# Zeros products on TensorE with other banks and other counts, in a one-core attention and MLP kernel

## The chip, the cores and the metric

The kernel runs on one core of a Trainium2 chip. The metric is the device time of one execution in microseconds (us); lower is better.

## What is computed

Eight batches of a Nyström attention (8 heads, 576 tokens, head dimension 64, 32 landmarks), followed by a two-layer MLP with squared ReLU over all 4608 tokens (512 to 2048 to 512). Cut to what matters:

```python
q_lm = q.reshape(B, H, m, S // m, D).mean(axis=3)      # m = 32 landmarks
k_lm = k.reshape(B, H, m, S // m, D).mean(axis=3)
A, Bm, C = sm(q, k_lm), sm(q_lm, k_lm), sm(q_lm, k)    # scaled softmax
Z = Bm.T / (norm1(Bm) * norminf(Bm) + 1e-6)
for _ in range(6):
    Z = 2 * Z - Z @ Bm @ Z
x = A @ Z @ C @ v                                      # as (tokens, 512)
out = np.maximum(x @ w_in, 0.0) ** 2 @ w_out
```

## The kernel before

A planner collects operations. Each operation has a number, the engines that it may run on, and what it reads and writes. A list written out by hand, `ORDER`, then says in which order they are emitted and on which engine; every engine works through its own part of the list in order. A table, `PACE`, adds a few waits to loads and to work on GpSimd (POOL). The batches are staged so that the attention of batch b + 1 is mixed with the MLP of batch b. The attention of batch 0 has no such partner, so in the first 40 us TensorE (PE) has little work of its own.

PSUM is one tile, `ps`, of eight banks of 512 float32 columns. A non-negative entry of `ORDER` is 64 times the operation's number, plus 8 times the engine, plus the first bank that the operation's PSUM result gets. A negative entry -(8n + bank) stands for n zeros products: PE multiplies a 128x128 tile of zeros by itself into the first 128 columns of that bank. Nobody reads the result. Where the bank holds a result that another engine has still to read, the zeros wait for that reader, as any other writer of the bank would; and since PE works in order, all that stands behind them on PE waits with them.

The names in the profile, for batch 0 (and 1), in the order of their work:

- `tr`, `trk` (line 579): transposes of q and k by a permutation, six at a time into one bank; the copy `trev` (lines 304 on ACT and 306 on VectorE, DVE) takes them to qT and kT.
- `l_sum` (544), `l_ev` (310), `l_fold` (554), `l_dup` (304): landmark sums, to qls, kls and then qdup, kdup.
- `bmq_0` (604): landmark scores. They go through `nmb` (619), `Eb` (626), BB, BTf, cs, `mx` (645), cc and rc on DVE and ACT; `p0_0` (660) makes a first product of them, from BTc.
- `c_mm` (759): scores of landmark queries and all keys, then `nmc` (765, the maximum on DVE), `c_exp` (769), `c_tr` (781), `c_ev` (304, to ECT), `cv` (803).
- `nv_0` (689) and `upd` (704): the six iterations for Z. PE makes the product, DVE the update `st`, and the next product needs that update.
- `a_mm` (873), `a_t` (884, to SA), `a_max` (888), `a_sub` (890), `a_exp`, `a_mul` (901): scores of queries and landmark keys, their softmax.
- `g_mm` (929) and its copies to G, then `in_mm` (948), `relu` and `square` (965 to 975), `o_mm` (1020): the MLP.

In the core's first 40 us the loads of q, k, v and the weights are issued by POOL, in part after a wait that `PACE` sets on a result of DVE.

The zeros products come from this function:

Of the kernel before, what the change touches and what calls it, by code (L numbers as in the profile page):

```python
# [40 lines left out]
    592, 32, 344, 280, 472, 720, -583, 2628, 2309, 160, 784, 408, 200, 88, -55, 2182, 2248, -78, 1607, 1664, 2696,  # L41
    1736, 2368, 2440, 2758, 1560, 1796, 1864, 2887, 2952, -47, 3013, 984, 2832, 6016, 3088, 3208, 3144, 1496, 2052,
    9734, 1927, 2120, 6096, 920, 2501, 2568, 1368, 1992, 6594, 1176, 3280, 3344, 856, 3408, 3536, 3464, -39, 4992,
    9476, 6672, 3600, 5072, 1048, 5128, 1112, 3781, 3664, 3728, 3920, 3856, 9544, 4738, 4816, 4872, -77, 3975, 4048,
    -71, 4101, 6160, 5252, 4176, 5192, 6736, 4936, 1240, 4231, 4304, -71, 4357, 536, 4432, 5520, 5584, 5320, 5383,
    6232, 8772, 6280, 6352, 4485, 1432, 6808, 5448, -31, 5632, 4560, 4615, 9800, 6416, 9157, 6480, 5712, 1304, 4688,
    5890, 5760, 6856, 6928, 6992, 7064, 9606, 5968, 9216, 5832, 7168, 7240, 6544, 7362, 7312, 7432, 7120, 8024, 7960,
    -87, 7552, 7696, 7496, 7624, 8455, 15170, 656, 15360, 8216, 8512, 15248, 15312, 9288, 9349, 9424, 15432, 8584,
    18328, 15554, 15744, 15632, 18456, 9680, 15496, 18392, 18264, 9031, 15816, 9096, 15896, 8645, -39, 7746, 7824,
    15936, 7880, 16008, 16088, 8848, 8902, 8976, 16130, 16208, 8712, 8280, 15688, 16320, 16392, 9863, 8088, 9936,  # L50
    9992, 10056, 13826, 13904, 16456, 16512, 16584, 13250, 10128, 10192, 10256, 8152, 10312, 10392, 10448, 10512,
    16264, 13328, 10576, 13968, 22980, 23040, 16648, 23104, 16704, 16898, 16776, 16968, 8344, 21573, 21632, 8408,
    13392, 10694, 16840, 23168, 10640, 10832, 17088, 17160, 17282, 17352, 24720, 23232, 23296, 10896, 18759, 10768,
    10950, 17032, 17472, 21696, 13464, 12098, 17544, 26000, 11024, 18816, 18880, 18944, 13512, 25232, 17224, 11088,
    11142, 25296, 12176, 12296, 12232, 14040, 14088, 11216, 12352, 12432, 12552, 19008, 19072, 19136, 21760, 21824,
    11280, 11334, 19200, 19272, 21888, 25360, 25552, 21952, 25424, 23360, 12488, 11408, 25616, 11472, 22016, 22088,
    11526, 13584, 24792, 17666, 17736, 11600, 12743, 12614, 14160, 12816, 17856, 11672, 11717, 17928, 23424, 17416,
    20167, 20224, 12688, 12994, 25688, 25752, 17608, 12880, 11792, 25496, 12944, 11920, 11856, 11974, 24400, 14224,
    13072, 18048, 12048, 13125, 20288, 23496, 18120, 25816, 25872, 13648, 17992, 13200, 20352, 14402, 14472, 14592,
    14664, 14296, 14352, 20416, 20480, 13720, 24472, 14544, 24856, 14786, 14728, 14920, 14856, 20544, 20608, 13776,  # L60
    31488, 24536, 25104, 23558, 24920, 22148, 24600, 23616, 23680, 14978, 24984, 31560, 24664, 25040, 20680, 15112,
    25168, 15048, 26048, 26128, 26192, 26312, 26248, 23744, 19333, 34648, 19392, 17816, 34776, 25936, 20743, 20800,
    34712, 22208, 31682, 31872, 26384, 18184, 31752, 31632, 26448, 26512, 26704, 31944, 26768, 19456, 19520, 18648,
    19584, 19648, 28354, 28432, 31816, 18584, 28480, 18712, 19712, 26568, 26648, 28560, 20864, 20928, 28624, 28872,
    28808, 19776, 28744, 23808, 26832, 20992, 19856, 20064, 19936, 34584, 23872, 23936, 26896, 24000, 34840, 21056,
    21120, 24080, 27024, 20000, 22272, 22336, 26949, 27088, 27152, 28680, 21184, 32064, 32136, 42960, 42128, 35078,
    35136, 27205, 27280, 32008, 32258, 22400, 32328, 32448, 43032, 21264, 42192, 27344, 29061, 29200, 29264, 32520,
    32200, 22464, 22528, 32392, 42256, 42320, 27399, 27472, 30146, 27544, 30224, 18520, 21344, 29568, 29648, 42648,
    22592, 22672, 32584, 29128, 28935, 35200, 35264, 35328, 30288, 32642, 32832, 20128, 27589, 27664, 42712, 27736,
    32712, 35392, 29712, 36420, 36480, 29784, 32904, 32776, 33026, 33096, 42512, 33216, 33288, 36544, 36608, 27781,  # L70
    36672, 33160, 33410, 27856, 33600, 33480, 35456, 43088, 27920, 27973, 32976, 33672, 36736, 36800, 33360, 33794,
    33736, 42384, 28048, 28176, 28112, 33864, 33984, 24288, 35520, 30360, 41816, 41880, 34056, 41944, 42008, 29008,
    42072, 35584, 29832, 43344, 35648, 28229, 28304, 29314, 29392, 29904, 21472, 22816, 30408, 30480, 21536, 29968,
    21408, 37767, 30544, 22880, 37824, 33544, 30040, 37888, 30616, 34176, 34370, 34248, 29445, 42576, 29512, 34440,
    34504, 35712, 22944, 22752, 36864, 36928, 37952, 42776, 36992, 30912, 30722, 31048, 30792, 33928, 30992, 39109,
    35776, 30864, 39168, 39232, 39296, 31296, 31368, 31432, 31106, 31240, 37056, 37120, 31176, 37184, 38016, 35840,
    38080, 34136, 30096, 30672, 48896, 42832, 34320, 37248, 38144, 43152, 42896, 43216, 35904, 51992, 43280, 38208,
    38272, 52184, 42448, 48968, 43458, 43536, 49032, 43600, 43720, 43656, 45760, 37312, 37376, 37448, 35032, 45840,
    34968, 43792, 43856, 43920, 43984, 44056, 38336, 35968, 36032, 36104, 39360, 45890, 45968, 44112, 46032, 46216,
    44176, 24224, 46280, 39424, 39488, 39552, 52120, 38400, 38464, 37600, 38528, 38592, 44240, 44304, 44356, 44496,  # L80
    46152, 46088, 39616, 39680, 39744, 39808, 37536, 52056, 39872, 49090, 49160, 39936, 40000, 44432, 44568, 44614,
    43408, 57880, 46468, 46536, 49280, 49474, 52376, 38656, 49352, 49544, 40064, 44688, 38720, 44752, 49232, 37664,
    44806, 24160, 36320, 44880, 44944, 59024, 49664, 47554, 38792, 47632, 47696, 24352, 40452, 40512, 40576, 49736,
    49800, 40136, 44998, 49856, 49928, 50050, 49432, 34904, 46343, 50120, 50184, 40640, 40704, 46976, 46608, 49616,
    45072, 45144, 37728, 49992, 53829, 50242, 50312, 47056, 53888, 53952, 47120, 46416, 46672, 50432, 50504, 45190,
    45264, 52440, 54016, 50376, 38944, 50626, 47768, 50696, 58704, 54080, 54144, 39008, 45328, 57936, 36192, 39072,
    58192, 50816, 38880, 50888, 45383, 45456, 45584, 45520, 54208, 40768, 40832, 50576, 47816, 51010, 51080, 50760,
    46720, 47184, 45638, 36384, 58008, 36256, 59096, 46800, 52487, 52544, 47240, 51202, 40288, 51392, 51464, 40896,
    51272, 58264, 47888, 47952, 40960, 41024, 41088, 58776, 45712, 46854, 54272, 41152, 51584, 47312, 58328, 59160,
    47376, 47448, 46928, 50952, 48322, 48400, 40352, 51656, 48456, 54336, 51144, 52608, 52672, 52736, 48512, 48584,  # L90
    48130, 48200, 52800, 47504, 48656, 48272, 51336, 40224, 41216, 41280, 41344, 58840, 48704, 48840, 58072, 48776,
    55174, 51778, 51848, 51912, 54400, 52864, 52928, 41408, 48024, 48080, 59224, 64960, 52992, 58136, 55232, 53056,
    65032, 58384, 58456, 58904, 58968, 58576, 59288, 51536, 65154, 53120, 65224, 40416, 59344, 58512, 53184, 68248,
    58640, 59520, 59600, 54464, 65096, 54528, 54592, 59664, 51736, 59784, 59720, 59856, 68184, 65346, 65416, 68120,
    54656, 54720, 41480, 55296, 41632, 65536, 41696, 54784, 65608, 68056, 65730, 65800, 54856, 59920, 55360, 59984,
    60048, 55008, 53248, 53312, 60176, 41760, 60112, 60420, 55424, 61824, 60240, 60304, 60368, 60560, 60496, 41568,
    61954, 55488, 55552, 65288, 55616, 56516, 61904, 55680, 55744, 55808, 55872, 62032, 62096, 62216, 62152, 60632,
    60677, 62344, 55936, 65496, 52248, 59472, 52312, 53376, 60752, 56576, 53440, 56640, 56704, 53512, 60816, 56000,
# [989 lines left out]
```

## Time and profile before

| | |
|---|---|
| median of 3 runs | 265.64 us (264.98 to 266.68) |
| profiled execution | 266.57 us, its span 264.9 us |
| PE busy | 249.0 us (94%), 3007 matmuls |
| weight loads | 148.8 us (56%) |
| DVE, ACT, POOL busy | 202.6 us (76%), 201.1 us (76%), 146.5 us (55%) |
| zeros products (line 455) | 138, busy 13.0 us, 6.4 us of PE's idle time just before them |
| granted PE clock, mean over the span | 0.981 |

The span runs from the first to the last instruction of the profiled execution; its time has 1.67 us more around it. PE is the busiest engine. The zeros are a small part of the instructions and lie between 1.06 and 36.6 us. The idle time before them is counted as idle time of PE, and the name behind it is that of the instruction that ended it.

### The profile page before, as it was taken

How to read it: one execution, taken by the hardware profiler on the slowest of the kernel's cores; microseconds unless marked ns; L12 is line 12 of the kernel's file. 1: busy time of each engine (PE TensorE's matmuls, PEld its weight loads, DVE VectorE, ACT ScalarE, POOL GpSimd, SP SyncE). 2: the span in 40 equal slices, each digit the busy share in tenths (PEclk: the TensorE clock that was granted, in tenths of full speed). 3: DMA queues.
4: the chain of work that ended last, by engine and by line, in shares of the span. 5: the costliest groups of instructions: out<-in, count | busy, mean ns of one | idle time of the engine just before them, and what ended most of it. 6: DMA issues, size and time to landing. Idle time of an engine off the chain costs nothing.

```text
span 264.9 us, 7773 instructions
## 1 busy us (share of the span) xinstructions
PE 249.0 (94%) x3007; PEld 148.8 (56%) x3046; DVE 202.6 (76%) x488; ACT 201.1 (76%) x417; POOL 146.5 (55%) x219
## 2 busy tenths in 40 slices
PE   8768979999999999999999999999999999999995
PEld 8756755444664456454655466545645556466552
DVE  0075879999999779879989789799998967944521
ACT  1566489997999798996899599886787878665510
POOL 7236577587568664856687573945555345531000
PEclk9995799999999999999999999999999999999999
DMA  6999899908940795069622993096503431012232
GB/s 159 210 167 158 134 192 207 178 4 134 201 98 4 118 247 109 0 89 194 104 59 40 185 166 105 2 162 120 120 15 46 79 96 42 0 43 64 66 118 84
DMA packets 20470, 28.60 MB, mean 108 GB/s; under 512 B 3280, under 2 KB 11728, under 8 KB 20432
## 3 DMA queue, kind: packets, MB, share of 16 engines
q0 software_dynamic: 13296, 18.06, 43.5%
q1 hardware_dynamic: 6848, 9.77, 12.8%
q8 instruction: 24, 0.39, 0.6%
q10 hardware_dynamic: 288, 0.26, 0.3%
q14 instruction: 14, 0.11, 0.1%
HBM read 36.70 MB, written 9.44 MB: 174 GB/s over the span
## 4 chain that ended last, share of the span: by engine, by line
PE 80%; DVE 7%; ACT 6%; POOL 4%; issue 3%; DVEq 0%; ACTq 0%
PE ps L1020 40%; PE ps L948 21%; PE ps L455 4%; PE ps L725 3%; PE ps L926 2%; PE ps L781 2%; PE ps L544 2%; POOL EA L901 2%; PE ps L803 2%; ACT r L965 1%; PE ps L694 1%; ACT kT L304 1%; PE ps L579 1%; DVE nmc L765 1%; POOL ks L512 1%
## 5 line engine op out<-in xcount | busy, mean ns | idle before, releaser
L1020 PE MATMUL ps<-w_out_bf,gs 128*128 128x512 bf16 (+1 forms) x553 | 139.1, 373 | 3.3 <-issue 2.2
L1020 PEld LDWEIGHTS <-gs 128*128 128x128 bf16 x592 | 53.5, 98 | 47.3 <-issue 8.1
L948 PE MATMUL ps<-AT,G 128*128 128x288 bf16 x512 | 78.9, 286 | 0.8 <-issue 0.3
L965 ACT ACTIVATE r<-ps 128x576 bf16<-128x576 f32 x108 | 68.1, 651 | 13.0 <-PE ps L948 10.9
L948 PEld LDWEIGHTS <-G 128*128 128x128 bf16 x512 | 48.7, 98 | 24.2 <-issue 1.1
L973 ACT ACTIVATE gs<-r 128x576 bf16<-128x576 bf16 x83 | 55.4, 682 | 4.1 <-DVE r L967 3.5
L975 POOL TENSOR_TENSOR gs<-r 128x576 bf16<-128x576 bf16 x22 | 25.2, 1152 | 18.6 <-DVE gs L975 9.4
L304 ACT CAST G<-ps 128x512 bf16<-128x512 f32 x47 | 24.8, 592 | 5.5 <-PE ps L926 3.1
L379 POOL DMA_DIRECT2D vraw<-in_v_dram x32 | 18.2, 571 | 17.3 <-DVE BTf L633 9.0
L304 ACT COPY o<-ps 128x512 f32<-128x512 f32 (+1 forms) x32 | 18.0, 569 | 11.6 <-PE ps L1020 11.6
L967 DVE TENSOR_SCALAR r<-ps 128x576 bf16<-128x576 f32 x20 | 15.2, 762 | 10.2 <-PE ps L948 7.9
L455 PE MATMUL ps<-zero 128*128 128x128 bf16 x138 | 13.0, 265 | 6.4 <-ACT kT L304 2.9
L638 POOL TENSOR_TENSOR Pd<-st,ones_d 128x256 bf16<-128x256 bf16 x17 | 11.4, 671 | 12.2 <-DVE st L704 8.6
L890 POOL TENSOR_TENSOR SA<-SA,mxA 128x576 f32<-128x576 f32 x12 | 13.9, 1162 | 7.2 <-DVE qs L512 3.8
L746 ACT ACTIVATE EC<-ps,nmc 128x288 bf16<-128x288 f32 x24 | 11.7, 500 | 7.9 <-DVE nmc L739 6.3
L901 POOL TENSOR_TENSOR EA<-EA,rA 128x576 bf16<-128x576 bf16 x13 | 15.0, 1159 | 2.5 <-DVE rA L899 1.2
L533 DVE STREAM_TRANSPOSE qT<-qraw 128x1152 bf16<-128x1152 bf16 x12 | 16.4, 1364 | 0.0
L533 DVE STREAM_TRANSPOSE kT<-kraw 128x1152 bf16<-128x1152 bf16 x12 | 16.1, 1348 | 0.0
L455 PEld LDWEIGHTS <-zero 128*128 128x128 bf16 x138 | 11.5, 121 | 7.7 <-issue 6.1
L704 DVE SCALAR_TENSOR_TENSOR st<-st,ps 128x128 bf16<-128x128 bf16 x40 | 11.2, 279 | 4.8 <-PE ps L689 2.2
L306 DVE CAST G<-ps 128x512 bf16<-128x512 f32 x17 | 11.2, 677 | 3.2 <-PE ps L929 2.3
L884 DVE STREAM_TRANSPOSE SA<-ps 128x576 f32<-128x576 f32 x16 | 12.0, 768 | 1.4 <-PE ps L725 0.9
(146 smaller groups left out, 365.4 us busy)
## 6 DMA issues: line engine op xcount, KB each, us to landing
out_dram<-o SPq DMA_DIRECT2D x126, 64.0 KB, 3.0
qraw<-in_q_dram POOLq DMA_DIRECT2D x16, 288.0 KB, 6.0
vraw<-in_v_dram POOLq DMA_DIRECT2D x32, 144.0 KB, 5.6
kraw<-in_k_dram POOLq DMA_DIRECT2D x15, 288.0 KB, 6.5
w_in_bf<-in_moe_w_in_dram POOLq DMA_DIRECT2D x4, 512.0 KB, 7.8
w_out_bf<-in_moe_w_out_dram POOLq DMA_DIRECT2D x4, 512.0 KB, 8.5
out_dram<-o SPq DMA_DIRECT2D x3, 256.0 KB, 2.1
gs<-in_k_dram SPq DMA_DIRECT2D x2, 288.0 KB, 4.2
```

The costliest lines, as they stand in the source:

```text
L304: nc.scalar.copy(dst, src)
L379: nc.gpsimd.dma_start(vraws[z][p0:p0 + 32, :, :, :].rearrange("p g t d -> p g (t d)"), src[b].rearrange(order, i=2, t=SEG)[i, :, :, c * NJ ...
L455: mm(ps[:, bank, 0:P], lhsT=zero[:], rhs=zero[:], start=True, stop=True)
L533: add("hx", "DVE", lambda e, nm=nm, raw=raw, i=i: nc.vector.transpose(heads(nm)[:, i, :, :, :].rearrange("p t h r -> p (t h r)"), raw[:, i ...
L890: keep("a_sub", add("a_sub", "DVE POOL", lambda e, part=part, spread=spread: ENG[e].tensor_tensor(part(SA), part(SA), spread(part(mxA)), A ...
L901: keep("a_mul", add("a_mul", "POOL DVE", lambda e, part=part, spread=spread: ENG[e].tensor_tensor(part(EA), part(EA), spread(part(rA)), AL ...
L948: mm(t[:, j, 0:HALF], lhsT=G[:, i, f * P:(f + 1) * P], rhs=AT[:, i, j * HALF:(j + 1) * HALF], start=(i == 0), stop=(i == 1))
L965: nc.scalar.activation(r.rearrange("p (j t) -> p j t", j=2), src, AF.Relu)
L967: nc.vector.tensor_scalar(out=r.rearrange("p (j t) -> p j t", j=2), in0=src, scalar1=0.0, scalar2=None, op0=ALU.max)
L973: nc.scalar.activation(dst, r[:], AF.Square)
L975: ENG[e].tensor_tensor(dst, r[:], r[:], ALU.mult)
L1020: mm(one(ok)[:, 0:hi - lo], lhsT=gs[:, f, x0:x0 + P], rhs=w_out_bf[:, f, lo:hi], start=(f == f0), stop=(f == f1 - 1))
```

## The change

Only the negative entries of `ORDER` change; all the other entries, 2100 of them, stand in the same order with the same engines and banks. `PACE` stays. There were 11 runs of zeros with 138 products, and there are 16 with 143. With the entries just before and behind each run, and what stands behind it:

```diff
   472, 720,
-  -583,      # 72 into bank 7
+  -479,      # 59 into bank 7
   2628,      # tr, q of batch 0
...
   200, 88,
-  -55,       # 6 into bank 7
+  -63,       # 7 into bank 7
   2182, 2248,   # trk into bank 6, its copy on ACT
-  -78,       # 9 into bank 6
+  -86,       # 10 into bank 6
   1607,      # l_sum of k
...
   2887, 2952,   # tr into bank 7, its copy on ACT
-  -47,       # 5 into bank 7
+  -52,       # 6 into bank 4
   3013,      # bmq_0
...
   3536, 3464,
-  -39,       # 4 into bank 7
+  -44,       # 5 into bank 4
   4992,      # c_mm
...
   5128, 1112,
+  -15,       # 1 into bank 7
   3781,      # p0_0
...
   4816, 4872,
   -77,       # 9 into bank 5, as before
   3975, 4048,   # nv_0, upd
-  -71,       # 8 into bank 7
+  -68,       # 8 into bank 4
   4101, 6160,   # nv_0, a_max
+  -23,       # 2 into bank 7
   5252, 4176,   # c_tr, upd
...
   4231, 4304,
   -71,       # 8 into bank 7, as before
   4357,      # nv_0
...
   6808, 5448,
-  -31,       # 3 into bank 7
+  -39,       # 4 into bank 7
   5632,      # cv
...
   8024, 7960,
-  -87,       # 10 into bank 7
+  -95,       # 11 into bank 7
   7552,      # g_mm
...
   15896, 8645,
-  -39,       # 4 into bank 7
+  -46,       # 5 into bank 6
   7746,      # g_mm
...
   8902, 8976,
+  -15,       # 1 into bank 7
   16130,     # in_mm
...
   9992, 10056,
+  -44,       # 5 into bank 4
   13826, 13904, # a_mm of batch 1, a_t
   16456,
+  -20,       # 2 into bank 4
   16512,     # in_mm
```

272 rows, old and new, of the table ORDER are left out of this document.

## The prediction

> **What bounds the kernel now.** I read the page's engine shares and its 40 slices first. TensorE (PE) is busy 94% of the span, and nearly all that it lacks lies in the first 44 us, where the zeros products run; behind that, windows of 4 us show it 92 to 100% busy. So time won in the start should move everything behind it forward. Then I read PE's instructions in order of time (start, length, group; in brackets the idle time before it and what ended it):
>
> ```profile
> 1.06 6.28 PE L455 MATMUL ps<-zero 128*128 128x128 bf16 x72 [1.06 <-DVE zero L464]
> 7.17 0.50 PE L579 MATMUL ps<-perm,qraw 128*128 128x128 bf16 x6
> ...
> 8.35 0.50 PE L579 MATMUL ps<-perm,kraw 128*128 128x128 bf16 x6
> 9.73 0.66 PE L455 MATMUL ps<-zero 128*128 128x128 bf16 x9 [0.89 <-ACT kT L304]
> ...
> 13.57 0.44 PE L455 MATMUL ps<-zero 128*128 128x128 bf16 x5 [0.89 <-ACT qT L304]
> 13.94 0.23 PE L604 MATMUL ps<-kdup,qls 128*32 128x32 bf16 x8
> ...
> 16.92 0.38 PE L455 MATMUL ps<-zero 128*128 128x128 bf16 x4 [1.04 <-ACT kT L304]
> 17.23 0.33 PE L759 MATMUL ps<-kT,qdup 64*32 64x288 bf16 x12
> ...
> 20.90 1.01 PE L455 MATMUL ps<-zero 128*128 128x128 bf16 x8 [0.46 <-DVE st L704]
> 21.84 0.29 PE L689 MATMUL ps<-st 32*32 32x64 bf16 x8
> ...
> 36.20 0.38 PE L455 MATMUL ps<-zero 128*128 128x128 bf16 x4 [0.98 <-ACT kT L304]
> ```
>
> To see: the zeros (L455) do not fill the idle time, they come after it. Each run waits until another engine has read its bank, and then delays the real product behind it. Next, the order of time of all engines, for who reads which bank:
>
> ```profile
> 12.38 0.37 ACT L304 CAST kdup<-ps 128x256 bf16<-128x256 f32 x1
> ...
> 12.72 0.80 ACT L304 COPY qT<-ps 128x768 bf16<-128x768 bf16 x1
> ...
> 15.10 0.80 ACT L304 COPY kT<-ps 128x768 bf16<-128x768 bf16 x1
> ...
> 16.04 0.83 ACT L304 COPY kT<-ps 128x768 bf16<-128x768 bf16 x1
> ...
> 17.65 0.76 DVE L765 TENSOR_REDUCE nmc<-ps 128x1 f32<-128x576 f32 x1 [0.65 <-PE ps L759]
> ```
>
> The run at 13.57 waits for the copy at 12.72 (bank 7), that at 16.92 for the copy at 16.04 (bank 7 again). Last, busy time and granted clock by stretches (PE busy is the number after the length; PEclk stands behind POOL), and the landing of the first q load, issued at 1.34 us:
>
> ```profile
> 8.88:12.30 3.42, 2.57 (x46) 2.56 (x46) 0.00 (x0) 2.25 (x4) 0.00 (x0) 1.00 1.12 207
> 12.30:15.71 3.41, 2.52 (x55) 1.93 (x52) 1.90 (x6) 2.31 (x8) 0.00 (x0) 1.00 1.19 208
> 15.71:19.12 3.41, 1.68 (x51) 1.16 (x44) 2.56 (x10) 1.98 (x7) 1.86 (x3) 1.00 1.00 146
> 19.12:22.54 3.42, 2.96 (x38) 2.38 (x37) 2.03 (x6) 2.16 (x7) 2.54 (x5) 0.50 0.99 125
> 25.95:29.36 3.41, 3.41 (x116) 2.88 (x109) 3.21 (x9) 1.33 (x3) 1.31 (x2) 0.50 0.68 118
> 29.36:32.78 3.42, 3.42 (x60) 2.41 (x58) 2.30 (x5) 2.34 (x5) 2.13 (x3) 1.00 1.09 166
> ```
>
> ```profile
> qraw<-in_q_dram POOLq DMA_DIRECT2D x1, 288.0 KB, 5.1
> ```
>
> The clock is halved from 19.12 to 29.36 us, right behind the stretch in which PE was busy for only 1.68 of 3.41 us (49%); 74% kept it.
>
> **The change part by part.** Order, banks of the real products and added semaphore waits stay; only zeros change, 138 to 143; no DMA is issued from another place. In the rows a zeros product costs 107 ns start to start up to about 5.4 us, and 56 ns after.
>
> (a) First run 72 to 59: the 13 that go are late ones, 13 x 0.056 = 0.73, so the transposes start at 6.45 instead of 7.17. Their data lands at 1.34 + 5.1 = 6.44: just in time. But the k transposes at 8.35 need a load issued at 2.07 that takes 5.8 us, 7.87. They start at 7.9: gain 0.45, less 0.06 for one zero more at 9.73 (same bank, same wait). **0.39.** The seventh zero of the second run lies in the wait for k.
>
> (b) Run at 13.57, bank 7 to 4: bank 4's reader is kdup, which ends at 12.75, and the product behind needs kdup anyway. Six zeros then end 0.34 + 0.05 later, at 13.14 instead of 13.94. **0.80.** Nmb, Eb and the rest of ACT and DVE follow.
>
> (c) Run at 16.92, bank 7 to 4: bank 4's reader ends at 15.90, and the scores behind need qdup (15.77 + 0.39 = 16.16). PE could start about 1 us earlier, but next late is DVE: nmc stands there behind a transpose and mx, which ends at 17.01, so nmc moves from 17.65 to 17.0. **0.65.** The new single zero behind it hides in the wait for BTc (17.01), which ACT makes after reading that bank; uncovered 0.06.
>
> (d) Run at 20.90, bank 7 to 4: it waited for the update that the next iteration needs too, so all eight lay on the path. Bank 4's reader (qT) ends at 19.75, so they run during the update. PE gains 0.94, but DVE has a_max (20.76 to 21.51) ahead of the next update, which moves from 22.18 to 21.51. **0.67.** The two new zeros behind hide in the wait for EC.
>
> (e) Runs at 19.10 (9) and 23.39 (8) keep bank and wait. Three and then four zeros ahead of cv end about when ECT does; DVE is later there anyway. The run of ten, now eleven, at 30.42 lies beside the G copy that ends at 31.13. Cost 0; the two extra zeros uncovered, 0.11.
>
> (f) Run at 36.20, bank 7 to 6: bank 7's reader ends at 36.14, bank 6's (DVE qT, 34.99 + 0.55) at 35.54. Gain 0.60 less one zero: **0.54.** ACT's and DVE's G copies were waiting for it.
>
> (g) Eight new zeros (1, 5, 2) after that: five lie in PE's idle 0.66 ahead of 39.72, two in the idle 0.31 ahead of 40.94, one beside a copy. Cost 0; uncovered 0.45.
>
> Waits: 0.39 + 0.80 + 0.65 + 0.67 + 0.54 = **3.05 us**.
>
> (h) The clock. The trace of before can't show whether it stays up. Between 12.30 and 20.14 PE is busy for 5.22 of 7.84 us; the same work, some 4.8 us with zeros at full speed, then fits in 5.8, 82%. The next 8.2 us hold 7.37 of busy time at half clock, about 4.4 at full, in some 6.8: 65%, between the 49% that lost the clock and the 74% that kept it, nearer the latter. So I take a full clock. Worth, on the path: nine zeros 1.01 to 0.50 (DVE has 0.7 idle there), eight at 23.39 the same way 0.47, transposes and sums from 28.37 to 29.86, 1.49 to about 1.05. **1.4**; bounds 0 (half clock as before) to 4 (half of the 7.37, if all were on the path).
>
> (i) The loads. Their issues follow DVE and move along, but the stream runs near 200 GB/s from 30 to 52 us and can only move into its holes: 16 to 18 us (118 GB/s, some 0.9 us lost) and 28 to 30 us (24 GB/s, 1.8 us). The q and k loads of the third batch land 1.9 and 2.6 us before they are used, so most of it is covered. I take **0.5** back; bounds 0 and 1.8.
>
> Sum: 3.05 + 1.4 - 0.5 = 3.95, so 264.9 becomes about 260.9. The profiled execution took 266.57 with 1.67 around the span, which would become 262.6. It lay 0.93 above the median of the runs (265.64), so against that median: 265.64 - 3.95 = **261.7**. A change under 1% (2.66 us) can hardly be told from none here.
>
> **The rivals.**
> *The half clock stays.* The longer fillings do not reach what keeps the clock; then 3.05 - 0.5 = 2.55 remain: 263.1. For it: 65% is untested. Against: the lull before 19.12 shrinks. The Trainium skill, "TensorE: Matmul & The Clock Gate", "What's actually happening", has the clock halved after an idle window of about 3.4 us; the trace disagrees, since it halves behind a window 49% busy. Its section "A second HAM failure mode: psum-queue depth-cycling" has small gaps between groups toggle the clock, which would make this rival likelier, and the trace bears that out.
> *The loads set the pace.* The stream moves only by its holes, 0.9 + 1.8 = 2.7: 262.9. For it: 193 to 211 GB/s between 36 and 48 us. Against: 1.9 us of slack before use.
> *Slower: the half clock moves later.* It decides if PE, now ahead, meets its thin stretch near 24 to 26 us, so that the three windows fall on the projections (L948, from 32 us before) instead of the small products. Those 10.2 us hold some 7.5 us of PE path work at full clock, which doubles, less 1.6 idle: +5.9. Only the waits' 3.05 is won: 265.64 + 2.85 = 268.5. Against: at half clock the projections fill PE fully, and one full window (25.95 to 29.36) brought the clock back.
> *The banks are not freer*, and the zeros wait as before: 265.6. Against: every new reader ends earlier in the rows above.
>
> **How the numbers follow.** Forecast 0.63, half clock 0.14, loads 0.12, slower 0.05, no effect 0.06. Faster by over 1% (under 263.0): forecast nearly whole (0.60), half of the two at 263 (0.13): 0.73. Slower by over 1%: 0.05. Between: 0.22. The range: below, a clock worth 1.9 more than taken and no loss to the loads, 259.3; above, the rivals near 263 and the 1.7 by which the runs of before lie apart, 264.8. No effect and slower stay outside.
>
> **What would show it.** Right: zeros directly behind the kdup copy, the k transposes at about 7.9, the first projection (32.04) near 28, a granted clock of 1.00 between 19 and 29 us. Wrong: idle time before L455 as long as now; a clock of 0.50 past 29 us; DMA waits on DVE's khalf or qT near 40 us.

## The result, and the profile after

The changed kernel took 262.37 us in the median of four executions (262.20 to 262.94); the kernel before took 265.31 us on the same chip (264.36 to 266.68). The ratio is 0.9889, with a 95% interval from 0.9842 to 0.9937: some 2.9 us faster, and the forecast was 261.7. The profiled execution took 262.38 us with a span of 260.7 us, against 266.57 and 264.9; its span is 4.2 us shorter, and the forecast's sum was 3.95. That the two profiles lie further apart than the medians is told below, under (h). Two single executions further down, of 980.72 and 1390.87 us, lie far outside all others and are left out of every mean and ratio.

PE after, in order of time, in the same columns as before:

```profile
1.06 6.22 PE L455 MATMUL ps<-zero 128*128 128x128 bf16 x59 [1.06 <-DVE zero L464]
7.12 0.50 PE L579 MATMUL ps<-perm,qraw 128*128 128x128 bf16 x6
...
8.35 0.50 PE L579 MATMUL ps<-perm,kraw 128*128 128x128 bf16 x6
...
12.87 0.49 PE L455 MATMUL ps<-zero 128*128 128x128 bf16 x6
13.29 0.23 PE L604 MATMUL ps<-kdup,qls 128*32 128x32 bf16 x8
...
15.29 0.44 PE L455 MATMUL ps<-zero 128*128 128x128 bf16 x5
15.66 0.33 PE L759 MATMUL ps<-kT,qdup 64*32 64x288 bf16 x12
...
18.53 0.62 PE L455 MATMUL ps<-zero 128*128 128x128 bf16 x8
19.08 0.24 PE L689 MATMUL ps<-st 32*32 32x64 bf16 x8
...
27.62 1.02 PE L948 MATMUL ps<-AT,G 128*128 128x288 bf16 x7
...
31.86 0.44 PE L455 MATMUL ps<-zero 128*128 128x128 bf16 x5 [0.38 <-DVE qT L306]
```

To see: the brackets ahead of the three runs that moved to bank 4 (12.87, 15.29 and 18.53) are gone. The zeros now lie in the time that PE would have idled, and bmq_0 (L604) starts at 13.29 instead of 13.94, the scores (L759) at 15.66 instead of 17.23, the second product of the iteration (L689) at 19.08 instead of 21.84. The run ahead of the last g_mm still waits, 0.38 instead of 0.98 us. But the first run, 13 zeros shorter, ends when the old one did: the transposes start at 7.12 (7.17 before) and those of k at 8.35 in both.

The granted clock by stretches, cut at the same times as before (PE's busy time stands behind the length, the clock behind POOL's):

```profile
15.71:19.12 3.41, 2.54 (x69) 1.93 (x72) 3.04 (x10) 2.53 (x8) 2.43 (x5) 1.00 1.09 162
19.12:22.54 3.42, 2.54 (x58) 2.00 (x58) 2.50 (x8) 2.85 (x9) 3.26 (x5) 1.00 1.06 135
22.54:25.95 3.41, 3.40 (x132) 2.59 (x131) 3.34 (x10) 1.49 (x4) 1.50 (x3) 1.00 1.19 196
```

The clock stays at 1.00 where it was halved from 19.12 to 29.36 us before. And a new wait, from the order of time of all engines:

```profile
29.17 0.61 PEld L544 LDWEIGHTS <-kraw 128*128 128x128 bf16 x9 [0.71 <-DMA kraw<-in_k_dram]
```

The bracket says that the weight load for the landmark sums of batch 1 waits for its k. That load was issued at 20.95 us instead of 23.44, but took 8.0 us to land instead of 5.3: 29.0 against 28.8 us. Whether k was really what PE waited for is taken up under (i) below.

### The profile page after: what moved, and what is told of

The parts are those of the page before. It is cut to its first block, busy times and chain, and to the rows that moved or that the text cites. A ratio compares the mean times of both kernels' runs of the same rounds, so it can differ in the third digit from the quotient of the medians.

```text
span 260.7 us, 7783 instructions
## 1 busy us (share of the span) xinstructions
PE 246.9 (95%) x3012; PEld 147.2 (56%) x3051; DVE 202.1 (78%) x488; ACT 201.1 (77%) x417; POOL 146.4 (56%) x219
## 4 chain that ended last, share of the span: by engine, by line
PE 79%; DVE 8%; ACT 4%; issue 4%; POOL 4%; DVEq 0%; ACTq 0%
PE ps L1020 40%; PE ps L948 21%; PE ps L455 4%; PE ps L725 3%; PE ps L926 2%; POOL EA L901 2%; PE ps L544 2%; PE ps L781 2%; PE ps L803 2%; PE ps L694 1%; DVE SA L884 1%; ACT r L965 1%; POOL ks L512 1%; PE ps L579 1%; DVE nmc L765 1%
## 5 line engine op out<-in xcount | busy, mean ns | idle before, releaser
L304 ACT CAST G<-ps 128x512 bf16<-128x512 f32 x47 | 24.8, 592 | 4.6 <-PE ps L926 3.1
L975 DVE TENSOR_TENSOR gs<-r 128x576 bf16<-128x576 bf16 x23 | 10.2, 450 | 3.5 <-ACT r L965 3.3
```

The source lines that it names most:

```text
L304: nc.scalar.copy(dst, src)
L975: ENG[e].tensor_tensor(dst, r[:], r[:], ALU.mult)
```

## The experiments

Runs of zeros are written as bank and count; an edit names the work that stands behind the run. All comparisons are with the kernel before on the same chip; a ratio is not exactly the quotient of the two medians beside it. The first four experiments ran on one chip, the next four on another, the last four on a third, and the changed kernel itself was not run again beside them. So where another kernel is set against the changed one, the ratios count more than the medians.

**All four bank moves, no count changed.**

```diff
-bmq_0: bank 7, 5    c_mm: bank 7, 4    second nv_0: bank 7, 8    last g_mm: bank 7, 4
+bmq_0: bank 4, 5    c_mm: bank 4, 4    second nv_0: bank 4, 8    last g_mm: bank 6, 4
```

> The kernel before with four runs of zeros moved to another bank and nothing else: the five ahead of bmq_0 and the four ahead of the first c_mm go to bank 4, the eight behind the first nv_0 to bank 4, the four ahead of the last g_mm of batch 0 to bank 6. All counts stay, 138 zeros. Theory (the waits are the gain): about 2.9 us less than before from the four runs, and the clock, if it stays at 1.00 with these counts, another 1; so 261.5 to 262.5 where before is 265.3. Rival (the counts, through the clock, are the gain): no more than 0.5 us, 264.8 or over, with a stretch of clock 0.50 as before.

Measured: 262.77 us, before 265.52; ratio 0.9893 (0.9849 to 0.9938). The banks alone bring nearly all of it, as the theory of the waits says; the median ended 0.3 above the expected stretch. The clock stayed up in all six executions.

**All counts and the new runs, old banks.**

```diff
 counts 59, 7, 10, 6, 5, 1, 9, 8, 2, 8, 4, 11, 5, 1, 5, 2 as in the changed kernel
-bmq_0: bank 4    c_mm: bank 4    second nv_0: bank 4    last g_mm: bank 6
+bmq_0: bank 7    c_mm: bank 7    second nv_0: bank 7    last g_mm: bank 7
```

> All counts and the five new runs of the changed kernel, but the four runs keep the bank that they had before (bank 7). Theory (the waits are the gain): PE idles about 1 us ahead of each of these runs, as before, and the time is 264.5 to 265.5, at most 0.4 us below before from the shorter first run. Rival (the counts are the gain): 262.4, like the changed kernel.

Measured: 264.65 us, before 265.52; ratio 0.9982 (0.9946 to 1.0017). Its PE rows (the list is a few lines longer here, so zeros stand at L464):

```profile
13.10 0.50 PE L464 MATMUL ps<-zero 128*128 128x128 bf16 x6 [0.89 <-ACT qT L313]
...
16.50 0.44 PE L464 MATMUL ps<-zero 128*128 128x128 bf16 x5 [1.04 <-ACT kT L313]
...
20.03 0.61 PE L464 MATMUL ps<-zero 128*128 128x128 bf16 x8 [0.46 <-DVE st L713]
...
33.07 0.44 PE L464 MATMUL ps<-zero 128*128 128x128 bf16 x5 [0.98 <-ACT kT L313]
```

The same waits as before, to the hundredth. More zeros behind such a wait fill nothing; the rival falls. The counts alone do not hold the clock either: it was halved in 4 of the 12 executions (mean clock 0.98 to 0.994).

**The changed kernel without the zeros between 16 and 23 us.**

```diff
-p0_0: 1   first nv_0: 9   second nv_0: 8   c_tr: 2   fourth nv_0: 8   cv: 4
```

> The changed kernel without the zeros ahead of p0_0, the first two nv_0, c_tr, the fourth nv_0 and cv (1 + 9 + 8 + 2 + 8 + 4 = 32 zeros left out). What the zeros are worth through the clock: if they hold the clock, a stretch at 0.50 comes back behind 19 us and the time is 1 to 3 us above the changed kernel (263.5 to 265.5). Rival: the clock holds without them, and since 17 of them lie on the path between an update and the next product, the time is 0.5 to 1 us below (261.5).

Measured: 262.58 us (262.00 to 262.98); ratio 0.9882 (0.9842 to 0.9921), the same as the changed kernel. Both guesses missed the size, and half of each was right. The clock by stretches:

```profile
12.75:16.16 3.41, 3.34 (x85) 2.41 (x86) 2.87 (x9) 2.83 (x9) 1.30 (x3) 1.00 1.18 208
16.16:19.58 3.42, 1.39 (x45) 0.81 (x41) 3.25 (x10) 2.79 (x10) 2.29 (x6) 1.00 1.06 169
19.58:22.99 3.41, 2.96 (x111) 2.48 (x112) 2.58 (x9) 3.04 (x6) 2.67 (x3) 0.50 1.08 145
22.99:26.40 3.41, 3.41 (x46) 2.25 (x44) 2.31 (x8) 0.42 (x3) 2.52 (x3) 0.50 1.23 205
```

With PE busy for 1.39 of 3.42 us the clock is lost, in every one of six executions (mean clock 0.985 to 0.993). But the 17 zeros ahead of the first and fourth nv_0 no longer stand in the path: the fourth update comes at 20.38 instead of 21.61 us (0.46 of that is there already at nmb), and this pays for the half clock. At the first projection this kernel, though 0.46 ahead at nmb, is behind (28.07 instead of 27.62 us). It wins that back near 29 us, where PE pauses in the changed kernel and not here (see (i)). So in these two traces the zeros hold the clock, and up to the first projection they bring more than they cost; at the end the two kernels are even.

**72 zeros in the first run of the changed kernel.**

```diff
-first run: bank 7, 59
+first run: bank 7, 72
```

> The changed kernel with 72 instead of 59 zeros in the first run. Theory: the 13 late zeros cost 0.056 us each while the clock is full, 0.7 us, of which the wait for the k load at 7.8 us takes back a part, so 0.3 to 0.7 us above the changed kernel (262.7 to 263.1). Rival: the moment at which the clock is granted decides alone, and the time is within 0.2 us of the changed kernel.

Measured: 263.27 us; ratio 0.9910 (0.9871 to 0.9950), 0.0021 above the changed kernel's, about 0.55 us. That lies in the expected stretch, but it does not show the theory: the two intervals overlap, and the four moves alone, which also begin with 72 zeros, had 0.9893 on this chip. In the profiled execution the clock was granted at 5.21 us; the transposes start at 7.05 and those of k at 8.28, no later than in the changed kernel (7.12 and 8.35), as the rival says. Its span is still 0.9 us longer (261.6), because PE pauses for 1.18 us near 28 us instead of 0.52 (see (i)) and then waits 0.7 us for w_out.

**Four more runs in free banks.**

```diff
-l_sum of k: bank 6, 10   first nv_0: bank 5, 9   fourth nv_0: bank 7, 8   cv: bank 7, 4
+l_sum of k: bank 0, 10   first nv_0: bank 7, 9   fourth nv_0: bank 5, 8   cv: bank 2, 4
```

> The changed kernel with four more runs of zeros in banks that nobody has still to read: the ten behind the first k copy go to bank 0, the nine ahead of the first nv_0 to bank 7, the eight ahead of the fourth nv_0 to bank 5, the four ahead of cv to bank 2. Theory (waits ahead of zeros are time on the path until the loads take over): the first projection comes 1 to 1.8 us earlier than in the changed kernel, but the load stream, which PE already waits for near 29 us, takes most of it back; the end is 0 to 0.6 us earlier (261.8 to 262.4). Rival (the loads only cost that one wait): the end is 1.2 to 1.8 us earlier (260.6 to 261.2).

Measured: 261.03 us (260.10 to 261.98); ratio 0.9839 (0.9797 to 0.9881). Its slowest execution is faster than the fastest of the changed kernel, though on another chip, and the intervals of the two ratios overlap; between the ratios lie 1.3 us, as the rival said. In the profiled execution the first projection starts at 25.89 instead of 27.62 us, and the end of the span moves from 260.7 to 258.3. PE shows no wait for a load here, and the pause near 29 us is not there either: that is 0.67 of the 2.4 us.

**A lighter load stream.** A part of v of batch 0 is not loaded, so its result is incomplete.

```diff
-load_v of batch 0: 4 loads of 144 KB
+load_v of batch 0: 2 loads of 144 KB, the tile zeroed once on DVE
```

> The changed kernel with two of the four loads of v of batch 0 left out (144 KB each; their part of v is zero, so a part of batch 0's result is left out). Some 1.4 us less work for the load stream at 200 GB/s. Theory (the stream caps the gain between 27 and 40 us): no DMA wait on PE in that stretch, and the end is 0.5 to 1.2 us before the changed kernel. Rival (the stream is hidden): the same time within 0.3 us.

Measured: 261.95 us; ratio 0.9879 (0.9839 to 0.9919), 0.0010 below the changed kernel's, about 0.3 us: the same, by the rival's measure. But PE was not free of loads, as the theory wanted: it waited 0.6 us for w_in and 0.7 us for w_out. So this run does not settle what the loads are worth.

**Both together.**

> Both of the above: the four more free banks and the lighter load stream (part of v of batch 0 left out). Theory (stream and waits in turn set the pace): here the free banks show their worth, 1.5 to 2.5 us below the changed kernel (260 to 261), and more below the light kernel alone than the free banks gain with all loads. Rival (free banks are worth nothing because DVE's chain is the pace): the same as the light kernel alone.

Measured: 261.21 us; ratio 0.9858 (0.9815 to 0.9900). No better than the free banks with all loads, and 0.7 below the light kernel; PE waited 1.0 us for w_out at 35.6 us. Leaving out 288 KB does not make the later loads land earlier than they are needed, so this edit did not do what it was to do.

**Free banks, and 50 zeros in the first run.**

```diff
-first run: bank 7, 59
+first run: bank 7, 50
```

> The kernel with four more free banks, and 50 instead of 59 zeros in the first run. The first q load lands at about 6.1 to 6.5 us. Theory: 59 zeros end between 6.0 and 7.6 us, as the clock happens to be granted early or late, so 50 remove the late cases: 0 to 0.3 us earlier than with 59, since the k load at 7.8 us and the load stream behind it still hold the rest. Rival: with fewer zeros the clock is granted a window later, PE runs at half speed up to 8.9 us or loses it near 19 us, and the time is 0.5 us or more above that with 59.

Measured: 261.36 us (260.24 to 262.52); ratio 0.9843 (0.9781 to 0.9905): no gain that shows over 59. Where PE waits in the profiled execution:

```profile
PE ps L929 <- DMA w_in_bf<-in_moe_w_in_dram: 1.6, 1, 1.6
PE ps L455 <- DVE zero L464: 1.1, 1, 1.1
PE ps L579 <- DMA kraw<-in_k_dram: 1.0, 1, 1.0
PE ps L579 <- DMA qraw<-in_q_dram: 0.8, 1, 0.8
```

PE reaches the q and k transposes before their data. And the third w_in load, issued at 17.2 us, lands at 27.1, while it landed at 24.8 when issued at 16.7 with 59 zeros. The same load took 9.9 us here and 8.1 there; with PE this far ahead such a difference becomes a wait, and it likely lies behind the spread of the time here.

**The four moves one by one, on the kernel before.** The first two together:

```diff
-bmq_0: bank 7, 5   c_mm: bank 7, 4
+bmq_0: bank 4, 5   c_mm: bank 4, 4
```

> The kernel before with two runs moved to bank 4 and nothing else: the five ahead of bmq_0 and the four ahead of the first c_mm. Theory (each wait is worth what its term said): 0.8 + 0.65 = 1.45 us below the executions of before with the same granted clock (264.7 at a clock of 1.00, 266.6 at 0.98), and in the trace nmc (17.65 before) 1.4 us earlier if PE starts as then. Rival (DVE's chain behind it gives it back): under 0.5 us.

Measured: 263.82 us, before 265.89; ratio 0.9948 (0.9916 to 0.9979). At a mean clock over 0.99 the executions average 263.6, before 264.8: 1.2 us of the 1.45. The profiled execution is the one of 980.72 us, so where nmc stands was not seen. The third:

```diff
-second nv_0: bank 7, 8
+second nv_0: bank 4, 8
```

> The kernel before with the eight zeros behind the first nv_0 in bank 4 instead of 7. Theory: 0.67 us below before at the same clock; in the trace the zeros start within 0.1 us of nv_0's end and the next update follows a_max without idle time on DVE. Rival: the softmax work on DVE and POOL sets the pace there, and nothing is gained.

Measured: 265.20 us; ratio 0.9997 (0.9966 to 1.0027). At a mean clock over 0.99, 264.8 against 264.8. The local part came true in kind: the second update starts 0.87 us after the first, right behind a_max. But it took 1.17 us with the old bank and a full clock (20.86 after 19.69 us in the experiment with the counts), so at full clock the move is worth 0.30 us, not 0.67. The interval of the ratio is 1.6 us wide, so the time can't show whether these 0.30 us reach the end. The fourth:

```diff
-last g_mm: bank 7, 4
+last g_mm: bank 6, 4
```

> The kernel before with the four zeros ahead of the last g_mm of batch 0 in bank 6 instead of 7. Theory: the idle time ahead of them falls from 0.98 to 0.38 us and the end comes 0.5 to 0.6 us earlier at the same clock. Rival: the loads for the second stage (36 to 52 us) hold the rest, and the end does not move.

Measured: 265.29 us; ratio 0.9985 (0.9953 to 1.0017); 264.8 at a mean clock over 0.99, as before. Where PE waits:

```profile
PE ps L455 <- DVE qT L306: 0.4, 1, 0.4
PE ps L929 <- DMA w_in_bf<-in_moe_w_in_dram: 0.4, 1, 0.4
PE ps L1020 <- DMA w_out_bf<-in_moe_w_out_dram: 0.3, 1, 0.3
```

The wait ahead of the zeros fell from 0.98 to 0.38 as expected, and in this execution two waits for weights stand in its place, as the rival says. The interval leaves room for the 0.5 us of the theory too, so the time decides nothing.

**Six more runs in free banks.**

```diff
-second nv_0: bank 4, 8   last g_mm: bank 6, 5
+second nv_0: bank 5, 8   last g_mm: bank 2, 5
```

> The kernel with four more free banks (measured at 261.03 us) and two more: the eight zeros behind the first nv_0 go to bank 5, the five ahead of the last g_mm of batch 0 to bank 2. Theory (waits are still the pace): the idle 0.25 and 0.38 us ahead of these two runs goes, 0.3 to 0.6 us below 261.0. Rival (the loads, whose landing times differ by up to 2 us from run to run, now set the end): 260.8 to 261.4, with a spread of 1.5 us or more.

Measured: 260.27 us (259.62 to 263.78); ratio 0.9829 (0.9778 to 0.9880), the fastest median here, though hardly below the four free banks by the ratio (0.9839). Four executions lie between 259.62 and 260.32, as the theory of the waits wants; two at 262.84 and 263.78, as the rival's spread wants. The profiled one is the 262.84. Its stretches:

```profile
33.20:36.62 3.42, 1.72 (x23) 1.01 (x24) 2.98 (x11) 3.20 (x10) 1.16 (x2) 1.00 1.18 211
36.62:40.03 3.41, 3.36 (x14) 1.77 (x14) 1.08 (x3) 1.37 (x3) 2.72 (x4) 0.50 1.11 211
```

PE waited 1.4 us for a w_out load, was busy for only 1.72 of 3.42 us, and then ran at half clock for 3.4 us over dense work. A late load costs twice here.

## Why the prediction was right, and where not

**(b), (c), the early waits: right.** In the two traces bmq_0 comes 0.65 us earlier (forecast 0.80 less one zero more on the way, which the first run was to pay for), and nmc 1.37, so another 0.72 (forecast 0.65).

**(d), the iteration: the mechanism right, the price partly the clock's.** The second update comes 0.76 us more forward than the first (0.67). But the 1.01 us for eight zeros was read where the clock was halved. From the first to the second update it is 1.63 us in the trace before, 1.17 with the old bank at full clock (all counts, old banks) and 0.87 with the new bank (the changed kernel). So the bank is worth 0.30 of it, and the clock the other 0.46.

**(a), the first run: right in the mean, wrong as a fixed price.** I cut 13 zeros at 0.056 us each, taking the clock to be granted at 5.4 us as in the one trace I had. In the profile after, it was granted at 6.88 us; more zeros ran at 107 ns, and the shorter run ended at the same time: nothing of the 0.39 came. In other executions here it was granted between 3.7 and 6.9 us. The Trainium skill says as much ("TensorE: Matmul & The Clock Gate", "What's actually happening"): the activity window of 3413 ns runs freely and doesn't start with the kernel. These traces agree: the stretches of half clock last 3.41, 6.83 or 10.24 us, one, two or three such windows. The k transposes start at 7.99 us in the mean of the seven traces with 59 zeros (7.71 to 8.35) and at 8.40 in that of the five with 72 (7.74 to 8.83), 0.4 us apart where I had 0.45; a single execution tells little.

**(h), the clock: the mechanism right, the term mis-sized both ways.** In the two traces the clock brought more than the 1.4 us: 0.46 between nmc and the first update (0.50), 0.47 at the fourth product (0.47), and 1.35 instead of 0.44 between the fourth update and the first projection. That last stretch takes 7.36 us before and 6.01 after, and 6.01 also with the second nv_0 alone, which has the old zeros there and a full clock. My term covered only its end, from 28.37 us on. Together that is 2.28, besides the 0.46 that I had put under (d).

Against the median I took too much, since I took the 1.4 us from an execution in which the clock was halved. In the 57 executions of the kernel before that stand beside the experiments, 26 have a mean clock under 0.99 and average 266.4 us; the other 31 average 264.7. So an execution with the half clock is 1.7 us longer, but fewer than half have it: that is worth about 0.8 on the average of all. In none of the 23 executions of the changed kernel, of the four moves alone, of the 72 zeros and of the four more free banks was the clock halved.

Set against its own profiled execution the sum was right to 0.25 us (3.95 for 4.2). That is partly luck: that execution ran at a mean clock of 0.981, like the 26, and there the 0.39 of (a) that did not come and the 0.88 that the clock brought beyond its term point in opposite ways. Against executions with a full clock my terms, with 0.30 for (d), give 0.39 + 0.80 + 0.65 + 0.30 + 0.54 - 0.5 = 2.18; the changed kernel's 262.4 lies 2.3 below 264.7, though not on the same chip.

**(i), the loads: the size close, but by luck, since the wait was most likely another.** I looked for it at the q and k of the third batch near 40 us. It came near 29 us: the work around it is 4.41 us earlier just ahead of that wait (DVE's first relu, 32.80 to 28.39) and 3.74 just behind it (ACT's, 33.22 to 29.48), 0.67 against the 0.5 taken. The bracket names k of batch 1. But PE stands still already at a matmul that doesn't read k, the first line below, and "issue" says that it waited for nothing that the profile shows. The others are the four moves alone, the 72 zeros and the second nv_0 alone (their source lines are numbered a little differently):

```profile
29.16 0.28 PE L948 MATMUL ps<-AT,G 128*128 128x288 bf16 x1 [0.52 <-issue]
29.36 0.77 PE L956 MATMUL ps<-AT,G 128*128 128x288 bf16 x5 [0.83 <-issue]
28.56 0.49 PE L553 MATMUL ps<-perm,kraw 128*128 128x128 bf16 x6 [1.18 <-issue]
29.39 0.77 PE L948 MATMUL ps<-AT,G 128*128 128x288 bf16 x5 [0.52 <-issue]
```

In the last three no wait for k is named. In all four, PE stops behind exactly 479 matmuls and 480 weight loads, and goes on 1.35 to 1.43 us after a block of 16 KB has landed on the DMA queue that the page calls "q8 instruction" (27.76 us in the changed kernel). In the other nine traces the 480th matmul comes 1.48 us or more behind that landing, and PE doesn't stop. So it most likely waited for its own instructions, and a kernel that is ahead, or has more zeros by then, runs into it. No run changed how instructions are fetched, so this is read from the traces and not tested. Loads do become waits elsewhere: PE waits for w_in or w_out with the lighter stream, with 50 zeros, with six more free banks and with the last g_mm alone.

**(f): right.** G's copies come 4.28 us earlier, so about 0.54 was won again, as forecast (0.54), and 4.2 us are left at the end of the span. With this move alone, no gain could be told from noise. **(e)** cost nothing: the 6.01 us from the fourth update to the first projection are the same with the old and the new counts. **(g)** cost 0.1 us at most, what is lost from 4.28 to the end.

**The first projection** moves by 4.42 us, to 27.62, the "near 28" of the forecast.

**The rivals.** The banks were freer, as the missing brackets show. The half clock did not stay. The loads most likely did not set the pace in the changed kernel. The half clock that moves later and lies over dense work did not come in it either, but it did in the kernel with six more free banks, by a late load and not by a thin stretch of PE's own.

## What to carry to other kernels

A filler does work only where it can start when the engine goes idle: look at the bracket ahead of it in the order of time, and if another engine's read ends the wait, give it a buffer whose reader is long done. A single profile is one draw of the clock and of the loads: before a stretch of half clock is put into a sum against a median, see in how many executions it is there, and price what lies in it at both clocks. And when the start of a kernel is tightened, check each load's landing against its new time of use, also those in between, since a stream that was hidden becomes the next wait. Look as well at idle time marked "issue": if it stands behind the same number of instructions in several kernels, it is no data that is late.

## What the runs showed of the hardware that I had not expected

The windows here are counted in steps of 3.413 us from the moment at which each trace shows the clock granted, up to some 50 us. The full clock was lost after the three windows in which PE was busy least: 1.39, 1.68 and 1.72 us, which is 41, 49 and 50%. It was kept after every other, down to 1.85 us or 54% (free banks with 50 zeros, first line below, the next window behind it) and 2.04 us or 60% (the last g_mm alone); the changed kernel's thinnest had 2.28 us, 67%. No window was empty. So in these traces the line lies between 50 and 54% busy, with a single window close by on either side.

```profile
24.27:27.68 3.41, 1.85 (x40) 1.03 (x40) 1.94 (x4) 1.66 (x4) 2.56 (x3) 1.00 1.13 180
27.68:31.10 3.42, 3.42 (x42) 2.89 (x39) 3.10 (x7) 2.63 (x6) 1.12 (x3) 1.00 1.09 156
```

Once the clock was halved, windows with PE busy for 87 and 88% at that clock (2.96 and 3.01 of 3.41 us) did not bring it back; windows at 98% (3.36) and 100% did.
